# A table of due times, columns of its own for every expert's list, and an earlier source for the early gather

## The chip, the cores and the metric

The kernel runs on one core of one Trainium2 chip. The metric is the device time of one execution in microseconds, as a median over runs. The core has five engines that run side by side and wait for each other by semaphores: TensorE (PE: matmuls), VectorE (DVE), ScalarE (ACT), GpSimd (POOL, which also issues the indirect DMAs) and SyncE (SP, which issues all other DMAs). Each works its instructions off in the order in which they were written.

## What is computed

Three stages, each on the output of the one before; 4 sequences of 768 tokens, 8 heads of 48 columns, all in float32:

```
for t in range(S):                                        # attention as a scan with complex decay
    S_re, S_im = (ar*S_re - ai*S_im + kv, ar*S_im + ai*S_re)
    y[:, :, t] = einsum('bhd,bhde->bhe', q[:, :, t], S_re)
x = x / rms(x) * rms_g                                    # dense layer, 3072 tokens, 384 -> 1536 -> 384
x = (silu(x @ w_gate) * (x @ w_val)) @ w_out
expert_idx = argmax(x @ w_gate2)                          # 8 experts, 384 -> 1024 -> 384, one for each token
for e in range(8):
    xe = x[expert_idx == e]
    out[expert_idx == e] = gate_w * (relu(xe @ w1[e]) @ w2[e])
```

## The kernel before

**Units.** The tokens go in 12 units of 256 (`U`, two chunks of 128). For each unit `elem` computes decays and phases (on ACT, DVE and POOL) and multiplies q and k by them; SP copies the result into `QK`, by heads; `attention` runs two chunks in `chunk`: scores, mask, state, output rows, their RMS factor (ten tiny operations on one column, L757 to L766) and a transpose into `xh` and `xl`, the high and low parts of the input of the dense layer. `dense` has 12 features, each a first step of 18 matmuls (L827), tanh on ACT, two products and a low part on DVE or POOL (L836 to L844), and a second step of 6 matmuls (L850) into two accumulators. `finish` stores the unit's rows and their 8 logits in `x2all` in DRAM (L882), finds each row's expert (L888 to L892, the one-hot `oh`), ranks the rows within their experts by matmuls (L899 to L902), and scatters each row's number into the lists `slots` (L921; one list for each chunk of a pair, so that two halves exist).

**Experts.** After unit 9 the largest expert so far is chosen as expert 0; its weights are loaded and split during the last unit. Half of its rows are taken *early*, from the rows known until then; the other half and the seven other experts, sorted by size, follow. `read_list` (L1059) loads both halves of a list from DRAM by SP and takes their minimum on DVE (L1068). `expert` gathers the rows by indirect DMAs on POOL (L1085), turns them (L1111), runs the first layer in 8 steps (L1129; results leave PSUM by ACT, L1136, and DVE, L1138, tile `ehl`; three PSUM banks), then the second (L1147), and scatters the results to the output by indirect DMAs on POOL (L1155), which read the same index tile. Weights of the next expert come through three raw buffers (SP, L1043 and L1045), split by ACT (L1050) and DVE (L1054) into h1, l1, h2, l2; two sets of weights alternate.

**The index tiles.** The early and the late list of expert 0 have tiles of their own; the seven others share three slots (L944), so that the list of expert 4 takes the place of expert 1's.

**The order.** `Plan` holds every step with the engines that can do it, its costs in us, its buffers and a due time. `issue` runs through a model of the five engines: it writes next the step that can start first, among equals the one that is due first, and so fixes the order on each engine. What a step costs, how long a result needs to land (`lag`) and when it is due (the numbers of `TUNE`) thus move instructions between places and, where a step has a choice, between engines; a negative number added to DVE's cost draws a step to DVE. `lock` marks steps of DVE and POOL that the model lets run one at a time.

## Time and profile before

| | us |
|---|---|
| median of 3 runs (lowest, highest) | 1008.8 (1007.71, 1011.72) |
| the profiled execution, its own time | 1006.66 |
| its span, first to last instruction | 1005.0 |
| TensorE busy (matmul) | 909.5 |
| VectorE, ScalarE, GpSimd busy | 642.2, 520.4, 197.5 |
| TensorE's granted clock, mean | 0.965 |

All rows come from the one profiled execution; 1.0 of granted clock is full speed. A wait in a row is the idle time of the engine just before an instruction, and the arrow names what ended it. The program falls into a start of some 75 us, the dense units to some 724 us, and the experts.

### The profile page before, as it was taken

What the parts mean: (1) busy time and instruction counts of PE and PEld (TensorE: products, weight loads), DVE (VectorE), ACT (ScalarE), POOL (GpSimd) and SP (SyncE); (2) the same over time, 40 slices, a digit from 0 to 9 for tenths busy, and PEclk for the clock granted to TensorE, in tenths of its full rate; (3) what the DMA queues carried; (4) which work ended last, traced back from release to release, by engine and by line L of the source; (5) the groups of instructions that cost most, each with busy time, mean ns of one, the idle gap of its engine ahead of it and who ended that gap; (6) DMA issues with size and microseconds to landing.
All of it is one profiled execution on the core that took longest, in us unless ns stands there. A gap on an engine that the chain in (4) does not pass through costs nothing. (4 is left out here: it accounts for less than half of the span.)

```text
span 1005.0 us, 18341 instructions
## 1 busy us (share of the span) xinstructions
PE 909.5 (91%) x6919; PEld 880.8 (88%) x6919; DVE 642.2 (64%) x1606; ACT 520.4 (52%) x1040; POOL 197.5 (20%) x265
## 2 busy tenths in 40 slices
PE   1869999999999999999989999999888968999994
PEld 1859999989999999899979999999878867999994
DVE  6899997777778696768577674655545523535510
ACT  8776766565646565646365652333325422534420
POOL 2244531020111101111000300000154112222111
PEclk9878999999999999999989999999999997999998
DMA  8835314423241515051505030012147413445301
GB/s 319 253 113 152 133 42 103 99 76 82 62 118 53 133 33 127 17 117 47 122 22 127 29 64 17 1 59 85 49 129 219 153 54 126 146 127 167 108 15 27
DMA packets 68639, 98.65 MB, mean 98 GB/s; under 512 B 16035, under 2 KB 49509, under 8 KB 68548
## 3 DMA queue, kind: packets, MB, share of 16 engines
q1 hardware_dynamic: 57860, 87.41, 30.8%
q0 software_dynamic: 10688, 10.04, 3.7%
q8 instruction: 55, 0.90, 0.4%
q14 instruction: 36, 0.29, 0.1%
HBM read 68.19 MB, written 10.55 MB: 78 GB/s over the span
## 5 line engine op out<-in xcount | busy, mean ns | idle before, releaser
L827 PE MATMUL m<-xh,w 128*128 128x256 f32 x1728 | 273.5, 286 | 8.5 <-DVE s L839 8.0
L827 PEld LDWEIGHTS m<-xh,w 128*128 128x128 f32 x1728 | 238.4, 193 | 10.7 <-DVE s L839 9.5
L850 PE MATMUL a<-wo,hh 128*128 128x392 f32 (+1 forms) x576 | 155.6, 351 | 1.6 <-ACT hh L842 1.1
L827 PE MATMUL m<-xl,w 128*128 128x256 f32 x864 | 151.1, 284 | 0.0
L827 PEld LDWEIGHTS m<-xl,w 128*128 128x128 f32 x864 | 124.7, 192 | 0.3 <-DVE xl L792 0.3
L834 ACT ACTIVATE s<-m 128x256 f32<-128x256 f32 x144 | 54.5, 381 | 100.1 <-PE m L827 58.5
L850 PEld LDWEIGHTS a<-wo,hh 128*128 128x128 f32 x576 | 98.7, 189 | 3.4 <-ACT hh L842 1.5
L850 PE MATMUL a<-wo,hl 128*128 128x392 f32 (+1 forms) x288 | 98.2, 341 | 0.0
L842 ACT ACTIVATE hh<-s 128x256 fp32r<-128x256 f32 x144 | 59.5, 416 | 71.1 <-PE a L850 56.8
L836 DVE SCALAR_TENSOR_TENSOR s<-s,m 128x256 f32<-128x256 f32 x144 | 59.2, 414 | 38.9 <-ACT s L834 38.6
L844 DVE TENSOR_TENSOR hl<-s,hh 128x256 fp32r<-128x256 f32 x144 | 65.6, 457 | 28.3 <-ACT hh L842 27.0
L1136 ACT ACTIVATE ehh<-m 128x384 fp32r<-128x384 f32 (+6 forms) x64 | 31.3, 490 | 60.4 <-PE m L1129 60.2
L1138 DVE SCALAR_TENSOR_TENSOR ehl<-m,ehh 128x384 fp32r<-128x384 f32 (+6 forms) x64 | 34.9, 554 | 40.3 <-ACT ehh L1136 40.1
L839 DVE SCALAR_TENSOR_TENSOR s<-s,m 128x256 f32<-128x256 f32 x144 | 59.3, 415 | 2.1
L1155 POOL DMA_INDIRECT out_dram<-eo,idxrest x24 | 30.8, 1282 | 137.6 <-ACT eo L1153 71.4
L1153 ACT ACTIVATE eo<-a,eg 114x384 f32<-114x384 f32 (+5 forms) x28 | 16.2, 580 | 78.1 <-PE a L1147 72.5
L921 POOL DMA_INDIRECT slots<-tid,sl x24 | 26.3, 1096 | 151.5 <-DVE cnt L916 147.8
L850 PEld LDWEIGHTS a<-wo,hl 128*128 128x128 f32 x288 | 54.1, 188 | 0.5 <-DVE hl L844 0.5
L665 PE MATMUL t<-QK 96*128 96x128 f32 x384 | 49.6, 278 | 0.0
L665 PEld LDWEIGHTS t<-QK 96*128 96x128 f32 x384 | 46.4, 192 | 1.2 <-issue 0.7
L1220 PE MATMUL a<-w,identr 128*128 128x384 f32 x96 | 22.6, 393 | 26.1 <-ACT w L411 24.1
L1220 PEld LDWEIGHTS a<-w,identr 128*128 128x128 f32 x96 | 19.9, 225 | 27.2 <-ACT w L411 24.6
(261 smaller groups left out, 1967.9 us busy)
## 6 DMA issues: line engine op xcount, KB each, us to landing
rawb<-in_w_dram SPq DMA_DIRECT2D x21, 512.0 KB, 4.1
rawb<-in_w_dram SPq DMA_DIRECT2D x28, 384.0 KB, 4.5
QK<-qk SPq DMA_DIRECT2D x24, 290.2 KB, 4.7
QK<-ee SPq DMA_DIRECT2D x24, 290.2 KB, 4.9
x2all<-x SPq DMA_DIRECT2D x13, 392.0 KB, 2.5
re<-in_a_re_dram SPq DMA_DIRECT2D x12, 384.0 KB, 3.8
im<-in_a_im_dram SPq DMA_DIRECT2D x12, 384.0 KB, 4.1
qk<-in_q_dram SPq DMA_DIRECT2D x12, 384.0 KB, 4.7
```

The lines of the kernel that those rows point to most:

```text
L665: TE.matmul(sc.t[:, i, :], lhsT=K(4 * g + i), rhs=Q(4 * g + i), start=True, stop=True)
L827: TE.matmul(ps.t[:, i, :], lhsT=W1[i, f * P // WB][k].t[:, part, fs], rhs=x.t[:, k, :], start=(n == 0), stop=(n == 3 * KD - 1))
L834: add((A, act(U)), lambda e: e.activation(s.t, ps.t[:, 0, :], AF.Tanh, scale=0.5), r=[ps], w=[s], due=dh, table=AF.Tanh)
L836: add((V, dve(U)), lambda e: e.scalar_tensor_tensor(out=s.t, in0=s.t, scalar=1.0, in1=ps.t[:, 0, :], op0=ALU.add, op1=ALU.mult), r=[s, ps] ...
L839: add((V, dve(U)), lambda e: e.scalar_tensor_tensor(out=s.t, in0=s.t, scalar=0.5, in1=ps.t[:, 1, :], op0=ALU.mult, op1=ALU.mult), r=[s, ps ...
L842: add((A, act(U)), lambda e: e.activation(hh.t, s.t, AF.Copy), r=[s], w=[hh], due=dh)
L844: lambda e: e.tensor_tensor(out=hl.t, in0=s.t, in1=hh.t, op=ALU.subtract), r=[s, hh], w=[hl], due=dh, lock=True)
L850: TE.matmul(acc[t].t[:, :wide], lhsT=h.t[:, ts_], rhs=WO[f].t[:, part, :wide], start=(f == 0 and n == 0), stop=(f == KF - 1 and n == 2))
L1136: add((A, act(N)), lambda e, f=f, ps=ps: e.activation(hh.t[:, f, :], ps.t, AF.Relu), r=[ps], w=[(hh, f)], due=d - 20)
L1138: add((V, dve(N)), lambda e, f=f, ps=ps: e.scalar_tensor_tensor(out=hl.t[:, f, :], in0=ps.t, scalar=0.0, in1=hh.t[:, f, :], op0=ALU.max, o ...
L1155: add((G, 1.05), lambda e, o=o, j=j: e.indirect_dma_start(out=out, out_offset=bass.IndirectOffsetOnAxis(ap=at(j), axis=0), in_=o.t, in_off ...
L1220: TE.matmul(fill.t, lhsT=identr, rhs=w.t[:, 0, :WB], start=True, stop=True)
```

## The change

- The nine lists (early, late, seven others) get columns of their own in one tile for each half; the three shared slots are gone.
- The early gather reads `x2all[:NT - U]` and depends in the plan on the rows of units 0 to 10 alone; the store of zeros into the last unit's rows at the start is gone.
- Costs in the plan: scan 1.92 us (from 6 times 0.20), phase 2.13, choose 1.0, place 0.7, tiny operations 0.1, totals and row copies 0.1 more; the lag of a scatter of numbers is 2.6 (from 2.0), of a gather 4.4 (from 2.2), of an output scatter 4.4 (from 2.0).
- All due times are new, and some choices: `RG=2` writes the ten tiny operations of units 0 and 1 as one step; `PE0`, `PE1` and the biases `MB`, `LB`, `RB`, `HB`, `EB` change which steps go ahead and whether DVE or POOL takes them.

```
-TUNE = dict(T0=143.38, PER=73.18, ..., PE0=0, PE1=0.45, RG=0, LB=0.29, EB=-1.55, RB=5.75, HB=-16.82, MB=1.05, ...
+TUNE = dict(T0=141.9, PER=75.64, ..., PE0=0.2, PE1=0, RG=2, LB=0.31, EB=-2.92, RB=13.33, HB=-12.38, MB=-0.22, ...
...
-    k_idx = {n: [Slots(e_right, f"idx{n}{i}", [P, NJ], I32, k) for i in range(NC)]
-             for n, k in (("early", 1), ("late", 1), ("rest", 3))}
+    k_idx = [Slots(e_right, f"idx{i}", [P, E + 1, NJ], I32) for i in range(NC)]
...
-    def read_list(name, x, lo, n, after):
-        both = [Buf(k, shape=[TPS[x], n]) for k in k_idx[name]]
+    lists = [Buf(k) for k in k_idx]
+    def read_list(x, row, lo, n, after):
+        at = [lambda b=b: b.t[:TPS[x], row, :n] for b in lists]
...
-                out=X.t[:, j, :], out_offset=None, in_=x2all,
-                r=[idx, X2ALL], w=[(X, j)], due=due(-30), lag=2.2, after=after)
+        rows, src = ([(X2ALL, u) for u in range(NU - 1)], x2all[:NT - U]) if rooms is rooms0 else ([X2ALL], x2all)
+                out=X.t[:, j, :], out_offset=None, in_=src,
+                r=[IDX] + rows, w=[(X, j)], due=due(-30), lag=4.4, after=after)
...
-        dma(lambda e: e.dma_start(x2all[NT - U:NT, :].rearrange("(c p) e -> p c e", p=P), zr.t),
-            U * XW * 4, r=[zr], w=[(X2ALL, NU - 1)], due=40)
```

**Expert 4's list, SyncE.** The place is expert 2's first layer. `rawb` are weight loads, `idxrest` a list load; DMASW are the semaphores of POOL's DMAs, DMAHW those of SP's. Before:

```order
L1043 DMA rawb_9759<-in_w_dram 128x1024 [waits DMAHW0_49,DVE_49]
L1064 ISA
L1064 DMA idxrest_9773<-slots_58 128x3 [waits DMASW6_49,DMASW7_49,DMASW5_49,DMASW4_49]
L1043 ISA
L1043 DMA rawb_9776<-in_w_dram 128x1024 [waits DMAHW1_49,DVE_49]
```

And in the changed kernel:

```order
L1041 DMA rawb_9760<-in_w_dram 128x1024 [waits DMAHW4_49,DVE_49]
L1041 ISA
L1041 DMA rawb_9775<-in_w_dram 128x1024 [waits DMAHW5_49,DVE_49]
L1041 ISA
L1041 DMA rawb_9806<-in_w_dram 128x1024 [waits DMAHW6_49,DVE_49]
```

The list load between the first two weight loads is gone; all lists now stand in the hand-over, some 70 rows earlier. On DVE, at the same place, the minimum goes from between two of expert 2's evictions:

```order
L1054 TENSOR_TENSOR l2b_9738<-rawb_9754,h2b_9729 128x768 [waits DMAHW2_49,Activation_49]
L1068 TENSOR_TENSOR idxrest_9773<-idxrest_9773,idxrest_9123 128x3 [waits DMASW7_49,DMASW6_49,DMAHW4_49,DMASW5_49,DMASW4_49]
L1138 SCALAR_TENSOR_TENSOR ehl_9756<-m_9781,ehh_9750 128x456 [waits Activation_49]
L1138 SCALAR_TENSOR_TENSOR ehl_9756<-m_9795,ehh_9750 128x456 [waits Activation_49]
L1138 SCALAR_TENSOR_TENSOR ehl_9756<-m_9814,ehh_9750 128x456 [waits Activation_49]
```

In the changed kernel `l2b` is followed by the evictions at once.

**The hand-over, TensorE.** The end of the last unit, where the ranking (`tri`, `ones`: L899 to L902) meets the early half of expert 0 (`h1a`, `l1a`). Before:

```order
L850 MATMUL a_8625<-wo_1846,hl_8822 128x392
L1111 MATMUL t_8848<-ident,x_8704 128x123 x2
L899 LDWEIGHTS ones
L899 MATMUL t_8865<-cnt,ones 128x8
L902 LDWEIGHTS tri
L902 MATMUL t_8865<-oh_8858,tri 128x8
```

In the changed kernel:

```order
L849 MATMUL a_8624<-wo_1764,hl_8821 128x392
L1132 MATMUL m_8852<-xh_8829,h1a_8288 128x246 x3
L1132 MATMUL m_8852<-xl_8841,h1a_8288 128x246 x3
L1132 MATMUL m_8852<-xh_8829,l1a_8292 128x246 x3
L1132 MATMUL m_8865<-xh_8829,h1a_8288 128x246 x3
L1132 MATMUL m_8865<-xl_8841,h1a_8288 128x246 x3
L1132 MATMUL m_8865<-xh_8829,l1a_8292 128x246 x3
L1132 MATMUL m_8886<-xh_8829,h1a_8288 128x246 x3
L1132 MATMUL m_8886<-xl_8841,h1a_8288 128x246 x3
L1132 MATMUL m_8886<-xh_8829,l1a_8292 128x246 x3
L898 LDWEIGHTS ones
L898 MATMUL t_8900<-cnt,ones 128x8
```

Three steps of nine matmuls now stand between the last dense matmul and the ranking.

**The start, VectorE.** The tiny operations of unit 0's second chunk (tile `rs`) among those of unit 1 (`ee`, `re`, `im`) and weight conversions (`raw`, `wo`). Before:

```order
L758 TENSOR_SCALAR rs_709<-rs_709 128x1
L532 COPY ee_666<-ee_666 128x3x2
L539 TENSOR_TENSOR ee_666<-ee_666 128x256 x3
L759 TENSOR_SCALAR rs_709<-rs_709 128x1
L406 SCALAR_TENSOR_TENSOR raw_354<-wo_216,raw_354 128x384
L761 TENSOR_TENSOR rs_709<-magic,rs_709 128x1
L401 SCALAR_TENSOR_TENSOR raw_496<-raw_496,wo_390 128x384
L762 TENSOR_SCALAR rs_709<-rs_709 128x1
```

In the changed kernel:

```order
L757 TENSOR_SCALAR rs_667<-rs_667 128x1
L758 TENSOR_SCALAR rs_667<-rs_667 128x1
L760 TENSOR_TENSOR rs_667<-magic,rs_667 128x1
L761 TENSOR_SCALAR rs_667<-rs_667 128x1
L763 SCALAR_TENSOR_TENSOR rs_667<-rs_667 128x1
```

The ten stand together, and unit 1's long operations behind them.

## Rows read from the trace of the kernel before

**Rows 1.** The page, busy tenths in 40 slices of 25.1 us: TensorE's total, TensorE, VectorE.
```profile
PE 909.5 (91%) x6919; PEld 880.8 (88%) x6919; DVE 642.2 (64%) x1606; ACT 520.4 (52%) x1040; POOL 197.5 (20%) x265
...
PE   1869999999999999999989999999888968999994
...
DVE  6899997777778696768577674655545523535510
```

**Rows 2.** TensorE's waits: line waited for, us in total, times, longest us.
```profile
PE m L1129 <- DVE ehl L1138: 16.9, 3, 12.8
PE m L827 <- DVE s L839: 8.0, 5, 3.8
```

**Rows 3.** TensorE's timeline (start us, us), and the window behind it (busy, PEclk).
```profile
833.60 1.51 PE L1129 MATMUL m<-exh,h1a 128*128 128x456 f32 x3 [12.79 <-DVE ehl L1138]
...
833.60:841.00 7.40, 7.40 (x24) 6.61 (x25) 1.91 (x4) 1.38 (x3) 2.92 (x3) 0.62 0.57 194
```

**Rows 4.** VectorE's timeline at that place.
```profile
832.84 0.16 DVE L1068 TENSOR_TENSOR idxrest<-idxrest,idxrest 128x3 int32<-128x3 int32 x1 [14.82 <-DMA idxrest<-slots]
```

**Rows 5.** SyncE's timeline at that place (issues alone).
```profile
812.97 0.35 SPq L1043 DMA_DIRECT2D rawb<-in_w_dram  x1
831.08 0.34 SPq L1064 DMA_DIRECT2D idxrest<-slots  x1
831.69 0.92 SPq L1043 DMA_DIRECT2D rawb<-in_w_dram  x2
```

**Rows 6.** POOL's timeline at that place.
```profile
823.15 1.64 POOL L1155 DMA_INDIRECT out_dram<-eo,idxrest  x1 [6.91 <-issue]
```

**Rows 7.** DMA issues, whole run: count, KB each, median us from issue to landing.
```profile
rawb<-in_w_dram SPq DMA_DIRECT2D x28, 384.0 KB, 4.5
...
ex<-x2all,idxrest POOLq DMA_INDIRECT x24, 7.5
out_dram<-eo,idxrest POOLq DMA_INDIRECT x24, 4.9
```

**Rows 8.** A window over later experts: us, then PE, PEld, DVE, ACT, POOL busy.
```profile
850.00:960.00 110.00, 110.00 (x638) 108.54 (x637) 50.53 (x92) 47.85 (x87) 25.95 (x22) 1.00 0.41 126
```

**Rows 9.** TensorE's timeline at the hand-over: its three waits.
```profile
725.59 0.17 PE L902 MATMUL t<-oh,tri 128*128 128x8 bf16 x1 [2.00 <-DVE oh L892]
...
747.05 1.73 PE L1111 MATMUL t<-ident,ex 123*128 123x123 f32 x6 [4.87 <-DMA idxrest<-slots]
...
760.25 0.63 PE L1129 MATMUL m<-exh,h1a 128*128 128x246 f32 x3 [3.37 <-DVE ehl L1138]
```

**Rows 10.** SyncE's and POOL's timelines at the hand-over: the late list and its first gather.
```profile
732.11 0.77 SPq L1064 DMA_DIRECT2D idxlate<-slots  x2
...
737.85 1.44 POOL L1085 DMA_INDIRECT ex<-x2all,idxlate  x1 [8.63 <-DVE idxrest L1068]
```

**Rows 11.** A window of early first-layer steps; a subtraction of weights on VectorE's timeline.
```profile
732.64:736.76 4.12, 4.12 (x37) 4.12 (x37) 2.76 (x16) 1.13 (x3) 0.00 (x0) 1.00 0.08 2
...
748.13 1.22 DVE L1054 TENSOR_TENSOR l1b<-rawb,h1b 128x1024 fp32r<-128x1024 f32 x1
```

**Rows 12.** TensorE's timeline, the first dense matmul.
```profile
75.18 1.09 PE L827 MATMUL m<-xh,w 128*128 128x256 f32 x3 [0.46 <-ACT xh L788]
```

**Rows 13.** VectorE's timeline, first and last of the second chunk's ten tiny operations.
```profile
67.02 0.15 DVE L758 TENSOR_SCALAR rs<-rs 128x1 f32<-128x1 f32 x1 [0.30 <-ACT y L753]
...
72.59 0.15 DVE L765 SCALAR_TENSOR_TENSOR rs<-rs 128x1 f32<-128x1 f32 x1
```

**Rows 14.** Groups by line: gain products (count, busy us, mean ns, idle before).
```profile
L586 DVE TENSOR_TENSOR ee<-qk,ee 128x768 f32<-128x768 f32 x24 | 23.5, 988 | 4.6 <-ACT ee L546 4.6
```

**Rows 15.** VectorE's and POOL's timelines at 58 us.
```profile
58.57 0.95 DVE L765 SCALAR_TENSOR_TENSOR rs<-rs 128x1 f32<-128x1 f32 x1
...
58.26 1.25 POOL L416 TENSOR_TENSOR w<-raw,w 128x384 fp32r<-128x384 f32 x1
```

**Rows 16.** Groups by line: the centring on POOL.
```profile
L539 POOL TENSOR_TENSOR ee<-ee 128x256 f32<-128x256 f32 x21 | 12.9, 639 | 51.5 <-DVE ee L532 51.5
```

More of the change, by code (lines that the diff above doesn't have):

```diff
@@ L28 @@
 TABLE_LOAD = 1.3
-TUNE = dict(T0=143.38, PER=73.18, FT=4.13, A0=68.94, A1=-49.43, A2=-21.78, E0=-117.9, E1=66.72, E2=94.44,
-            E3=115.52, CG=0.23, CO=255.09, LC=-54.51, NRAW=6, AHEAD=6, DH=22.42, FI=-69.19, RP=-13.39, TOL=0,
-            S2L=47.73, NS=3, NH=3, HOP=0.2, W1=133.05, ATP=2, PA0=0, PA1=0, PE0=0, PE1=0.45, RG=0, LB=0.29,
-            EB=-1.55, RB=5.75, HB=-16.82, MB=1.05, TB=25.48, AX=1, EE=-32.55, EL=7.09, BEG=0.7, DL=2, FN=8,
-            FF=23)
+TUNE = dict(T0=141.9, PER=75.64, FT=4.32, A0=71.68, A1=-61.52, A2=-18.6, E0=-150.88, E1=65.4, E2=78.3, E3=75.68,
+            CG=8.52, CO=243.96, LC=-56.68, NRAW=6, AHEAD=6, DH=24.1, FI=-65.62, RP=-25.83, TOL=0, S2L=45.45,
+            NS=3, NH=3, HOP=0.2, W1=131.99, ATP=2, PA0=0, PA1=0, PE0=0.2, PE1=0, RG=2, LB=0.31, EB=-2.92,
+            RB=13.33, HB=-12.38, MB=-0.22, TB=26.62, AX=1, EE=-22.83, EL=9.31, BEG=0.7, DL=2, FN=8, FF=23)
 HOP = TUNE["HOP"]
@@ L527, in scan @@
                                          initial=0.0, op0=ALU.add, op1=ALU.subtract)
-        at((V, 6 * dve(C)), scan, r=[ta, tb], w=[(ee, "m")], lock=True)
+        at((V, 1.92), scan, r=[ta, tb], w=[(ee, "m")], lock=True)
         at([(G, pool2(N3)), (V, dve(N3))],
@@ L735, in keep_rows @@
                     e.tensor_copy(yT[s], yt.t[s])
-            at([(A, act(4 * C)), (V, dve(4 * C))], keep_rows, r=[yt], w=[(YT, n)])
+            at([(A, act(4 * C)), (V, dve(4 * C) + 0.1)], keep_rows, r=[yt], w=[(YT, n)])
         def turn_rows(e):
@@ L910, in place @@
             e.tensor_copy(sl.t, mx.t)
-        add((V, 0.9), place, r=[rk, oh], w=[t1, mx, sl], due=due)
+        add((V, 0.7), place, r=[rk, oh], w=[t1, mx, sl], due=due)
         def count(e):
@@ L1057, in load_weights @@
         return W
-    def read_list(name, x, lo, n, after):
-        both = [Buf(k, shape=[TPS[x], n]) for k in k_idx[name]]
+    lists = [Buf(k) for k in k_idx]
+    def read_list(x, row, lo, n, after):
         due = due_e(x, -30)
-        for x_, sl in zip(both, slots):
-            dma(lambda e, x_=x_, sl=sl: e.dma_start(x_.t, sl[bass.ds(which[x] * NT + lo, n * TPS[x]), :].rearrange(
-                "(p j) o -> p (j o)", j=n)), 2e3, r=[SLOTS], w=[x_], due=due,
-                after=after + [told[x]])
-        a, o = both
-        add((V, 0.1), lambda e: e.tensor_tensor(out=a.t, in0=a.t, in1=o.t, op=ALU.min), r=both, w=[a], due=due)
-        return a
+        at = [lambda b=b: b.t[:TPS[x], row, :n] for b in lists]
+        for b, t, sl in zip(lists, at, slots):
+            dma(lambda e, t=t, sl=sl: e.dma_start(t(), sl[bass.ds(which[x] * NT + lo, n * TPS[x]), :].rearrange(
+                "(p j) o -> p (j o)", j=n)), 2e3, r=[SLOTS], w=[(b, row)], due=due, after=after + [told[x]])
+        a, o = at
+        add((V, 0.1), lambda e: e.tensor_tensor(out=a(), in0=a(), in1=o(), op=ALU.min),
+            r=[(lists[1], row)], w=[(lists[0], row)], due=due)
+        return row
     begun = []
@@ L1078, in expert @@
         N = n * TP
+        rows, src = ([(X2ALL, u) for u in range(NU - 1)], x2all[:NT - U]) if rooms is rooms0 else ([X2ALL], x2all)
+        IDX = (lists[0], idx)
         def at(j):
-            return idx.t[:, j:j + 1]
+            return lists[0].t[:TP, idx, j:j + 1]
         X, g = Buf(k_x, shape=[TP, n, XW]), Buf(k_g, shape=[TP, n, E + 1])
@@ L1157, in expert @@
                 in_=o.t, in_offset=None, bounds_check=NT - 1, oob_is_err=False),
-                r=[o, idx], due=d, lag=2.0)
+                r=[o, IDX], due=d, lag=4.4)
     with tc.manual_schedule():
@@ L1240 @@
             if u + 1 == NU:
-                early = read_list("early", 0, 0, NE, [to_right])
+                early = read_list(0, 0, 0, NE, [to_right])
                 expert(0, Wn, early, NE, rooms0, lambda i: due_e(0, i) - TUNE["EE"], [to_right])
@@ L1251 @@
         add((V, 2.0), sort, r=[MORE, HOT], w=[PERM], due=due_moe(NU, 0) - 60)
-        late = read_list("late", 0, EARLY, NJ - NE, [to_right])
+        late = read_list(0, E, EARLY, NJ - NE, [to_right])
         expert(0, Wn, late, NJ - NE, rooms, lambda i: due_e(0, i), [to_left])
@@ L1255 @@
             W = load_weights(x_, [to_left])
-            idx = read_list("rest", x_, 0, NJS[x_], [to_right])
+            idx = read_list(x_, x_, 0, NJS[x_], [to_right])
             expert(x_, W, idx, NJS[x_], rooms, lambda i, x_=x_: due_e(x_, i), [to_left])
```

10 lines of the change are left out of this document (5 added, 5 removed).

## The prediction

> **What bounds the kernel now.** I read the page first. TensorE is busy for 909.5 of 1005.0 us, and the slices show where it isn't: at the very start, in slices 29 to 34 (the hand-over to the experts) and in the last [rows 1]. TensorE bounds the kernel and its matmuls are the same before and after, so the question is which of its idle stretches go and which come. The table of its waits names them by releaser [rows 2]: 12.8 us in one piece behind a VectorE eviction `ehl` (L1138); the dense steps' waits for evictions are 8.0 us in five, the longest 3.8.
>
> I followed the 12.8 us back, engine by engine. TensorE's timeline has it at 820.81 to 833.60, in the first layer of expert 2 (456 rows) [rows 3]: three PSUM banks are full, and VectorE doesn't empty them. VectorE's timeline says why: it stood for 14.82 us at L1068, the minimum of the two halves of expert 4's list, whose second half had not landed, with the evictions queued behind it [rows 4]. SyncE issued that list load at 831.08, though its previous instruction was at 812.97; two weight loads then followed at once, so they had waited behind it [rows 5]. POOL's timeline gives the cause: the last scatter of expert 1 went out at 823.15 for 1.64 us [rows 6], a scatter lands 4.9 us after its issue in the median [rows 7], and until then the index tile that it reads can't be overwritten. That list takes the slot of expert 1 (three slots for seven lists). So **the chain is scatter landing, list load, minimum, eviction, matmul**, and nothing in it is arithmetic. After the wait the granted clock is 0.62 in the mean of 833.60 to 841.00, between the levels of 1.2 and 2.4 GHz [rows 3].
>
> **Term 1, own columns.** The nine lists get columns of their own. In the order of the changed kernel no list load waits for a scatter (their waits are all on SyncE's own rings), and expert 2's evictions have no minimum between them. The wait goes whole: 12.79 us, and with it 7.4 x (1 - 0.62) = 2.8 us of slow clock [rows 3], together **-15.6 us**. What is late next here? The weight loads of expert 4, which stood behind the list; they now follow their own buffers, which VectorE frees before it reaches the place of the old wait. From 850 to 960 the same pattern, with shorter list waits, leaves TensorE busy for 110.00 of 110.00 us [rows 8]; I take that as what this stretch is without the stall. Bounds: -15.6, and -11 should one weight load's landing, 4.5 us [rows 7], show in its place.
>
> Here the Trainium skill weighs in ("DMA: Bandwidth & Descriptors", section on the anatomy of a DMA from GpSimd): such a DMA costs about 2.0 us fixed plus its bytes. By it the list would have been free at some 826.8, four us sooner, and the term would be an estimate of -11.5. The trace disagrees: 4.9 us for a scatter, and 7.5 us for a gather [rows 7].
>
> **Term 2, the hand-over.** Dense work ends at 723.59. TensorE then waits 2.00 us for the one-hot [rows 9], ranks, and SyncE reads the late list at 732.11; POOL starts the late gathers at 737.85 [rows 10], and TensorE, out of early work, stands still until 747.05 [rows 9]. Now three steps of the early expert (27 matmuls) stand ahead of the ranking. A stretch of 36 such matmuls takes 4.12 us [rows 11], so they take 3.1 us and cover the wait. But the ranking comes 1.1 us later, and so may the gathers. TensorE has 12 second-layer matmuls more done when it meets the late turn, 1.4 us at the 0.114 us of rows 11 and more as they are longer; but nothing then covers the eviction of the turned rows. I take -2 us: the wait for the one-hot, the rest against each other. The 3.37 us wait at 760.25 [rows 9] is again VectorE in order (expert 1's gate, which waits for a gather, ahead of evictions); two evictions now stand ahead of that gate: -1 us. Bounds of both: -10.2 (all three waits go) and +3.5 (three subtractions of expert 1's weights, 1.22 us each [rows 11], now stand ahead of the late rows' low part, where one did). Term: **-3 us**.
>
> The early gather reads `x2all[:NT - U]` and the zero fill of the last unit's rows is gone. The gather was already ordered after unit 10 alone, so I cost this at nothing; what covers the gather is the last unit's dense work, and without it some 7.5 us of landing [rows 7] would show. The last unit's row store no longer waits for it, and it wasn't late.
>
> **Term 3, the start.** The first dense matmul runs at 75.18, 0.46 us after its input [rows 12]. That input waits for the ten tiny RMS operations of the second chunk, which VectorE spread over 67.02 to 72.74 between long ones [rows 13]. With RG=2 the ten stand together: 10 x 0.15 = 1.5 us instead of 5.7, **4.2 us** sooner. Moreover the work of unit 1 ahead of the first dense eviction shrinks, three gain products (L586) fewer alone: 3 x 0.99 = 3.0 us [rows 14]. Both only defer work of VectorE, which is busy for 90% or more of slices 3 to 6, until 150 us [rows 1]; so most is given back. Bounds -9 (all kept) and +3 (unit 1's preparation, now later, stops attention). Term: **-3 us**.
>
> Here a rule speaks against the change. Beside a POOL subtraction from 58.26 to 59.51 a one-column VectorE operation (L765) took 0.95 us [rows 15], which elsewhere takes 0.15 [rows 13]. The changed order has seven such subtractions (L416) on POOL before unit 1's factors, not four. The Trainium skill ("SBUF — State Buffer", section on who interferes with whom) has it that a VectorE operation with two SBUF inputs and a GpSimd one that reads SBUF exclude each other for a whole instruction. By that rule three more of the row's 1.25 us take up to 3.8 us from VectorE (an estimate), and term 3 would be some +0.8. The row agrees, in one place; how often the two meet is not seen in it, so the term stays and its bound holds this.
>
> **Term 4, the middle.** In six units the centring `middle` (L539) moves from POOL to VectorE: 18 instructions of 0.64 us there [rows 16], at most 11.5 us onto VectorE, which has 6 to 8 tenths to do in those slices [rows 1]. Fewer matmuls stand between a unit's last turn of y and its first dense step: counted in the order, 174 in unit 6 before (and attention besides), 54 now. That is less reserve, not a wait. I take **0**; below, all of the 8.0 us of rows 2 could go, above, as much could come.
>
> Of the planner's other numbers (durations of scan, totals, gates, lags) none adds an instruction; they act through the order alone, and are in the terms above. The tail, three scatters one after another behind the last matmul, stands in the same order: 0.
>
> **Sum.** -15.6 - 3 - 3 + 0 = -21.6 us against the profiled execution's 1006.66 us: 985.1. The median of the runs shown is 1008.8, 2.1 us above that execution: **987 us**.
>
> **The rivals.** *Stall only* (0.28): the order's other moves cancel. Then 1008.8 - 15.6 = 993. For it: terms 2 and 3 are small, and each has a bound on the other side. *More than I count* (0.10): the three hand-over waits go whole (-10.2 for -3) and the start keeps 6 of its 9 us: 987 - 7 - 3 = 977. *The wait moves* (0.07): all seven later lists are now loaded during the hand-over, between weight loads that wait for VectorE, and their minima stand on VectorE ahead of the late half's evictions. If a list sits behind a weight load as it did before, TensorE pays one wait of rows 3 again: 993 + 15.6 = 1008. Against it: no scatter is in that chain now. *Slower: attention late at every unit* (0.06): the reserve ahead of units 3 to 6 falls to 18 to 60 matmuls (at 0.114 us some 2 to 7 us), VectorE has `middle` besides, and the first step then waits for xl. At the 3.8 us of rows 2 six such stops in eleven units give 993 + 23 = 1016; it is slower from the sixth on, and with four about even. For it: VectorE is in order, and one late operation has that price. Against it: no present wait of that kind shows. *It doesn't do what it says* (0.01): should the columns of one tile be treated as one buffer, list loads would still wait for scatters. The order shows they don't. The forecast itself has 0.48.
>
> A measurement of this kernel can't tell less than about 0.5% (5 us) from no change. Faster by more: 0.48 + 0.28 + 0.10 = 0.86; within: 0.07 + 0.01 = 0.08; slower: 0.06. The range must drop no more than 2 in 10: I leave out the two cases at 1008 and above and the far end of the bounds below (-15.6 - 10 - 9 = -35 gives 974), and hold the forecast, the stall-only case and its bound of -11 with +3.5 of term 2 (about 1001): 975 to 1002.
>
> **What would show it.** In the changed profile: no list load later than the hand-over and no VectorE wait of over 3 us for one; expert 2 without a gap, clock 1.00 throughout the experts (term 1). No wait for the one-hot, and the turn of the late rows still waiting 3 to 6 us (term 2). The first dense matmul at 66 to 71 us (term 3). Waits of the dense steps for evictions of 0 to 16 us together (term 4). Wrong, if TensorE's idle time between 760 and 960 stays over 10 us, or if waits for xh or xl appear at the starts of units.

## The result and the profile after

| | before | changed |
|---|---|---|
| median of 4 runs (lowest, highest), us | 1008.25 (1003.58, 1011.72) | 975.51 (974.43, 980.38) |
| ratio, 95% interval | | 0.9688 (0.9636, 0.9739) |
| span of the profiled execution, us | 1005.0 | 972.7 |
| TensorE busy, us | 909.5 | 901.4 |
| TensorE idle: 0 to 100 us / 100 to 700 us / 700 us to the last matmul / tail | 35.7 / 22.0 / 25.0 / 12.8 | 42.2 / 6.4 / 9.9 / 12.8 |

The change takes 33 us, where the forecast had 22; the new time lies half a microsecond inside the lower end of the stated range. The last row of the table is the one to read: it is each stretch less TensorE's busy time in it, from the windows below. The start became worse, the units lost nearly three quarters of their idle time, and the experts lost 15 us. TensorE's busy time also fell by 8.1 us for the same 6919 matmuls. That is the granted clock: 1.00 for 0.99 in the units and 0.97 for 0.96 behind them, in the windows below. These busy times are those of one execution each, and executions of one and the same kernel differ in their clock too (last section).

The page of the changed kernel, where the lines of [rows 1] stand now:

```profile
PE 901.4 (93%) x6919; PEld 877.0 (90%) x6919; DVE 642.2 (66%) x1612; ACT 527.8 (54%) x1050; POOL 186.4 (19%) x249
...
PE   0867999999999999999999999999987999999994
...
DVE  5889897858787868786968586646545543554510
...
PEclk9978899999999999999999999999997999999998
```

Windows of the changed kernel (stretch, then PE, PEld, DVE, ACT, POOL busy with counts, granted clock, DMA share, GB/s):

```profile
0.00:100.00 100.00, 57.79 (x394) 54.69 (x394) 82.83 (x165) 73.26 (x134) 33.87 (x74) 0.88 0.60 196
100.00:700.00 600.00, 593.61 (x5085) 580.35 (x5085) 444.28 (x1210) 349.57 (x724) 78.81 (x119) 1.00 0.31 77
700.00:959.90 259.90, 249.96 (x1444) 242.01 (x1442) 115.07 (x238) 104.39 (x191) 71.49 (x54) 0.97 0.42 123
765.00:835.00 70.00, 70.00 (x382) 66.59 (x381) 31.92 (x51) 29.63 (x50) 17.09 (x14) 1.00 0.46 141
```

And of the kernel before:

```profile
0.00:100.00 100.00, 64.35 (x457) 60.50 (x458) 85.05 (x179) 75.85 (x144) 32.84 (x70) 0.88 0.66 208
100.00:700.00 600.00, 577.95 (x4914) 561.77 (x4914) 435.86 (x1172) 333.97 (x691) 88.05 (x138) 0.99 0.29 74
700.00:992.20 292.20, 267.20 (x1552) 258.49 (x1550) 121.31 (x256) 110.00 (x204) 74.33 (x57) 0.96 0.38 112
```

In the first 100 us the changed kernel runs 63 matmuls fewer, though VectorE is nearly as busy (82.83 us for 85.05). From 100 to 700 us it is the other way round: 171 more, at full clock. From 765 to 835 us, where the 12.8 us stood [rows 3], TensorE is never idle.

TensorE's waits in the changed kernel (line waited for, us in total, times, longest), against [rows 2]:

```profile
PE a L1221 <- POOL w L412: 25.1, 1, 25.1
PE t L781 <- ACT y L776: 7.3, 5, 5.0
PE m L826 <- ACT w L410: 5.1, 1, 5.1
PE m L1132 <- DVE ehl L1141: 4.0, 2, 3.2
...
PE m L826 <- DVE s L838: 0.5, 2, 0.3
```

The first line is the idle time ahead of the first matmul (19.8 us before). The dense steps' waits for evictions fell from 8.0 to 0.5 us. New are a wait of 5.0 us for `y` and one of 5.1 us for a dense weight, both in the start. The hand-over in TensorE's timeline, against [rows 9]:

```profile
727.32 0.30 PE L1114 MATMUL t<-ident,ex 123*128 123x123 f32 x1 [2.70 <-DMA idx<-slots]
729.21 1.29 PE L1114 MATMUL t<-ident,ex 123*128 123x123 f32 x5 [1.59 <-DMA ex<-x2all,idx]
...
741.49 1.00 PE L1132 MATMUL m<-exh,h1a 128*128 128x246 f32 x3 [3.20 <-DVE ehl L1141]
```

The wait for the one-hot is gone, the late turn waits 4.3 us in two pieces (4.87 before), and the wait for `ehl` is 3.20 us (3.37 before).

### The profile page after: what moved, and what is told of

It is laid out like the page before. It is cut to its first block, busy times and chain, and to the rows that moved or that the text cites. A ratio compares the mean times of both kernels' runs of the same rounds, so it can differ in the third digit from the quotient of the medians.

```text
span 972.7 us, 18324 instructions
## 1 busy us (share of the span) xinstructions
PE 901.4 (93%) x6919; PEld 877.0 (90%) x6919; DVE 642.2 (66%) x1612; ACT 527.8 (54%) x1050; POOL 186.4 (19%) x249
## 5 line engine op out<-in xcount | busy, mean ns | idle before, releaser
L826 PE MATMUL m<-xh,w 128*128 128x256 f32 x1728 | 276.3, 286 | 6.0 <-ACT w L410 5.1
L843 DVE TENSOR_TENSOR hl<-s,hh 128x256 fp32r<-128x256 f32 x144 | 62.3, 437 | 33.5 <-ACT hh L841 32.9
L835 DVE SCALAR_TENSOR_TENSOR s<-s,m 128x256 f32<-128x256 f32 x144 | 59.0, 414 | 36.0 <-ACT s L833 35.3
L1158 POOL DMA_INDIRECT out_dram<-eo,idx x28 | 37.6, 1344 | 152.0 <-ACT eo L1156 47.1
L664 PE MATMUL t<-QK 96*128 96x128 f32 x384 | 52.0, 279 | 1.7 <-DMA QK<-ee 1.7
L1221 PE MATMUL a<-w,identr 128*128 128x384 f32 x96 | 21.7, 382 | 27.4 <-POOL w L412 25.1
L1221 PEld LDWEIGHTS a<-w,identr 128*128 128x128 f32 x96 | 19.3, 217 | 27.9 <-POOL w L412 25.1
```

Source lines behind the costliest of these rows:

```text
L664: TE.matmul(sc.t[:, i, :], lhsT=K(4 * g + i), rhs=Q(4 * g + i), start=True, stop=True)
L826: TE.matmul(ps.t[:, i, :], lhsT=W1[i, f * P // WB][k].t[:, part, fs], rhs=x.t[:, k, :], start=(n == 0), stop=(n == 3 * KD - 1))
L835: add((V, dve(U)), lambda e: e.scalar_tensor_tensor(out=s.t, in0=s.t, scalar=1.0, in1=ps.t[:, 0, :], op0=ALU.add, op1=ALU.mult), r=[s, ps] ...
L843: lambda e: e.tensor_tensor(out=hl.t, in0=s.t, in1=hh.t, op=ALU.subtract), r=[s, hh], w=[hl], due=dh, lock=True)
L1158: add((G, 1.05), lambda e, o=o, j=j: e.indirect_dma_start(out=out, out_offset=bass.IndirectOffsetOnAxis(ap=at(j), axis=0), in_=o.t, in_off ...
L1221: TE.matmul(fill.t, lhsT=identr, rhs=w.t[:, 0, :WB], start=True, stop=True)
```

## The experiments

The order on each engine is fixed when the kernel is written, so it can be recorded. In six kernels below (start_before, units_before, experts_before, loads_first, first_30us_before, weights_swapped) the plan doesn't choose: the changed kernel is written in a given list of steps, each with its engine. At step 740 (some 165 us) and at step 2660 (some 665 us) the two orders have done the same steps but for three and for none, so that they can be joined there. This is the edit (`ORDER` is the list; the ten tiny operations of units 0 and 1 are single steps in it):

```
+        turn = [(self.steps[int(w.rstrip("."))], w.endswith(".")) for w in ORDER]
         left = len(self.steps)
         while left:
             cand = []
-            for s in ready:
+            for s, other in turn:
+                if s.wait:
+                    continue
...
-                for e, c, *bias in s.engs:
+                for e, c, *bias in [s.engs[other]]:
```

| kernel | median (lowest, highest), us | ratio to before (95%) | idle, as above | TensorE busy |
|---|---|---|---|---|
| own_columns | 992.43 (988.18, 995.83) | 0.9827 (0.9794, 0.9860) | 34.2 / 23.9 / 13.4 / 12.2 | 910.0 |
| start_before | 970.94 (970.09, 973.21) | 0.9627 (0.9600, 0.9653) | 33.9 / 9.3 / 10.9 / 12.5 | 902.3 |
| units_before | 1002.97 (998.80, 1006.82) | 0.9924 (0.9896, 0.9952) | 41.4 / 22.4 / 13.1 / 12.6 | 912.1 |
| experts_before | 977.15 (975.57, 981.42) | 0.9692 (0.9663, 0.9722) | 42.4 / 6.8 / 12.9 / 12.3 | 900.6 |
| due_times_only | 1016.48 (1013.17, 1021.26) | 1.0079 (1.0049, 1.0108) | 36.6 / 21.1 / 30.0 / 12.2 | 913.4 |
| durations_only | 1001.07 (999.18, 1002.33) | 0.9915 (0.9891, 0.9940) | 35.3 / 12.5 / 24.6 / 12.9 | 913.5 |
| old_due_times | 985.11 (980.68, 985.42) | 0.9745 (0.9717, 0.9774) | 41.1 / 14.9 / 15.0 / 12.1 | 900.3 |
| loads_first | 992.34 (990.51, 997.08) | 0.9845 (0.9815, 0.9874) | 33.9 / 22.0 / 14.9 / 12.5 | 905.6 |
| scan_phase_only | 984.38 (983.73, 988.43) | 0.9796 (0.9772, 0.9821) | 39.0 / 18.1 / 14.3 / 12.0 | 899.4 |
| small_costs_only | 1003.34 (998.02, 1008.24) | 0.9962 (0.9941, 0.9984) | 40.7 / 22.9 / 13.7 / 12.5 | 912.6 |
| first_30us_before | 980.97 (979.74, 983.96) | 0.9753 (0.9732, 0.9774) | 41.4 / 8.7 / 11.0 / 12.3 | 904.7 |
| weights_swapped | 977.71 (975.37, 982.11) | 0.9708 (0.9687, 0.9729) | 42.6 / 7.3 / 12.2 / 12.7 | 905.6 |

The kernel before stood beside the first four at 1009.57 us (median), beside the next four at 1009.55, beside the last four at 1007.32. Differences between two of these kernels are taken from medians, and the spread within one kernel says that under some 4 us they mean little. The ratios are not ratios of the medians, and a difference taken from them can come out some 5 us otherwise; where that matters, both are given. Idle and busy times are those of one profiled execution.

### own_columns

```
+        if s.name.startswith("idxrest"):
+            if not hasattr(s, "whole"):
+                s.whole, s.row = s.where[0].tile([s.shape[0], 7, s.shape[1]], s.dtype, name=s.name, tag=s.name, bufs=1), 0
+            self.t = s.whole[:self.shape[0], s.row, :self.shape[1]]
+            s.row += 1
+            return
```

This stands in `Buf.place` of the kernel before: the plan still counts three slots and makes the same order, only the buffers differ.

> The kernel before, with the order of every engine unchanged; only the seven later lists get columns of their own, so that no list load has to wait for a scatter. Theory (term 1 is the own columns alone, whatever the order): the wait of 12.8 us at the first layer of expert 2 goes with its slow clock, 1008.3 - 15.6 = 992.7 us, within 2.5; TensorE's idle time from 763 us to the last matmul under 1 us. Rival (the list load then waits in SyncE's queue behind a weight load, or the weight load is what is late): the wait shrinks to 4 to 12 us and the time is 997 to 1008. Second rival (the order of the change is needed for the gain): 1005 or more.

Measured: ratio 0.9827, which is 17 us off (14 to 21 by the interval). The two kernels can be laid beside each other from the matmul behind the wait for `ehl` in the hand-over to the last one, 1227 matmuls in the same order. The kernel before, then own_columns:

```profile
760.25:992.20 231.95, 218.35 (x1227) 211.57 (x1227) 93.58 (x164) 89.33 (x158) 52.48 (x41) 0.96 0.38 116
```

```profile
764.20:981.60 217.40, 216.10 (x1227) 210.50 (x1227) 94.37 (x164) 90.22 (x158) 53.20 (x41) 0.99 0.41 123
```

TensorE is idle for 1.3 us there, one wait at 787 us, where it was idle for 13.6 before. From 763 us on, the stretch of the expectation, it is 2.5 us with the end of the wait for `ehl`, not under 1. List load and minimum stand where they stood. The stretch is 14.6 us shorter, 12.3 us of it idle time and 2.3 us clock, against 12.8 and 2.8 in term 1. That is a better measure of term 1 than the 17 us: the spans of the two profiled executions differ by only 11.2 us, since this execution of own_columns came to the stretch 4 us later, and the kernel's six runs lie in two groups, 988.2 to 990.4 and 994.5 to 995.8 us, with the median between them. So term 1 is the buffers alone, the order of the change isn't needed for it, and in this order nothing took the wait's place.

### units_before

`ORDER` is the change's up to step 740, that of before from there to step 2660, the change's behind it.

> The changed kernel, whose steps 741 to 2660 (units 2 to 10, some 165 to 665 us) are written in the order of the kernel before; start, hand-over and experts as in the change. Theory (the due times of the units, not the lists, bring the larger part: idle 16.4 us less and the clock's loss of some 5.8 us gone): 975.5 + 20 = 995 us, within 4, with the two waits of 3.8 and 2.5 us for evictions near 500 and 527 us back. Rival (the units gain because of how the start leaves VectorE): 975 to 983. Second rival (half of each): 983 to 991.

Measured: 1002.97 us, 27 us slower than the change (24 by the two ratios), more than any theory had. Both waits are back:

```profile
515.30 0.62 PE L986 MATMUL m<-xh,w 128*128 128x256 f32 x3 [4.21 <-DVE s L998]
537.47 1.01 PE L986 MATMUL m<-xh,w 128*128 128x256 f32 x3 [2.53 <-DVE s L998]
```

The spans differ by 28.9 us: idle time by 18.1 (16.0 of it in the units, 3.2 behind them), busy time by 10.8 (912.1 against 901.4). **The order of units 2 to 10 is the largest part of the change**, and over a third of what it is worth is clock: in the kernel before, the 3.8 us stop at 502 us is followed by nine microseconds at a mean granted clock of 0.69, between its levels of 1.2 and 2.4 GHz, without any idle time in them:

```profile
506.00:515.00 9.00, 9.00 (x66) 8.58 (x67) 5.05 (x13) 6.01 (x10) 0.00 (x0) 0.69 0.00 0
```

Busy time doesn't follow idle time in every kernel, though: durations_only (below) is idle for 10 us less than the kernel before and busy for 4 us more.

### experts_before

`ORDER` is the change's up to step 2660, and that of before from there, lists included (they have own columns here too).

> The changed kernel, whose last 893 steps (the last unit, hand-over and experts) are written in the order of the kernel before, with the lists in columns of their own. Theory (the order at the hand-over is worth little: idle time of 9.9 us against 11.4 before, same clock): 975.5 + 1.5 = 977 us, within 2.5. Rival (ranking behind three steps of the early expert and the lists loaded early are worth what term 2 allowed): 980 to 986. Second rival (own columns need the early loads): a wait of over 4 us in the experts, 982 to 990.

Measured: 977.15 us, 1.6 us slower than the change, less than the runs tell apart; TensorE's idle time behind 700 us is 3.0 us more. The wait for the one-hot (2.00 us) and the late turn's 4.89 us are back, and little else:

```profile
700.00:962.70 262.70, 249.76 (x1456) 241.98 (x1454) 115.86 (x241) 104.61 (x193) 72.19 (x54) 0.99 0.42 123
```

### start_before

`ORDER` is that of before up to step 740, and the change's behind it.

> The changed kernel, whose first 740 steps (the start and units 0 and 1, to some 165 us) are written in the order of the kernel before, all later ones in the order of the change. Theory (the changed start is worse: its idle time to 100 us is 42.2 us against 35.7, with about 1 us more of slow clock): 975.5 - 7.5 = 968 us, within 3. Rival (a start only moves work of VectorE: what it gains is given back before 300 us): 973 to 977. Second rival (the gain of the later units comes from what the changed start does ahead): slower than the change, 980 or more.

Measured: 970.94 us, as the theory had it and faster than both kernels by medians (its interval and the change's, 0.9600 to 0.9653 and 0.9636 to 0.9739, overlap a little; the three kernels with the changed units and the changed start, in weights_swapped but for two conversions, are at 975.5 or over). So the changed start costs about 5 us. The loss, in the stretch from 60 to 100 us, of start_before:

```profile
60.00:100.00 40.00, 32.53 (x265) 30.67 (x262) 38.99 (x90) 27.14 (x59) 13.51 (x18) 0.80 0.45 122
```

and of the changed kernel:

```profile
60.00:100.00 40.00, 25.63 (x163) 24.17 (x163) 38.84 (x82) 24.34 (x52) 14.61 (x19) 0.74 0.31 100
```

VectorE is full in both (39 of 40 us), but TensorE does 102 matmuls fewer in the changed order. Its waits say what differs. In the kernel before, 18 turns of output weights (`wo`) stand ahead of the first dense matmul, and TensorE waits for two conversions among them, 5.9 us in all (start_before has the same two waits):

```profile
69.87 0.47 PE L439 MATMUL t<-identr,wo 128*128 128x128 f32 x1 [3.50 <-POOL wo L413]
72.73 1.33 PE L439 MATMUL t<-identr,wo 128*128 128x128 f32 x5 [2.39 <-DVE wo L416]
```

In the changed kernel 6 such turns stand there; TensorE now waits for `y` and `xl` instead, 6.6 us in all:

```profile
66.62 0.90 PE L781 MATMUL t<-ident,y 128*128 128x128 f32 x3 [4.97 <-ACT y L776]
70.73 1.10 PE L826 MATMUL m<-xl,w 128*128 128x256 f32 x3 [1.66 <-DVE xl L791]
```

The waits for conversions come all the same, behind the first dense matmul: 5.07 us, shown next, and 1.52 us at 99 us. So the idle time of this stretch (14.4 us against 7.5) grew by about what the waits for `y` and `xl` are.

### weights_swapped and first_30us_before

The changed kernel's 5.07 us wait, followed back: TensorE's row, and ACT's ahead of it, of the changed kernel.

```profile
95.47 0.58 PE L826 MATMUL m<-xh,w 128*128 128x256 f32 x1 [5.07 <-ACT w L410]
...
91.94 1.28 ACT L580 ACT_TABLE_LOAD   x1
...
93.35 0.92 ACT L581 ACTIVATE ta<-ta,halfpi 128x768 f32<-128x768 f32 x1
94.17 0.83 ACT L589 ACTIVATE re<-re 128x768 f32<-128x768 f32 x1
94.91 0.51 ACT L410 ACTIVATE w<-raw 128x384 fp32r<-128x384 f32 x1
```

A dense weight's high part stands on ACT behind unit 1's cosine and sine. Two conversions were exchanged in `ORDER` (steps 213 to 218 and 248 to 253):

```
+m = {249: 214, 248: 213, 250: 215, 251: 216, 252: 217, 253: 218}
+m.update({v: k for k, v in m.items()})
+ORDER = [(m.get(q, q), other) for q, other in ORDER]
```

> The changed kernel in its own order, but two conversions of dense weights change places in it: the one for which TensorE waits 5.07 us at 95 us goes into the places of the one that stands ahead of it and is due later (so it gets its scratch buffer some 10 us sooner, and its last step on ACT stands ahead of unit 1's cosine with its table load, not behind). Theory (this one late conversion is most of what the changed start loses): the wait goes to under 1.5 us, 975.5 - 4 = 971.5 us, within 2. Rival (the next conversion is then late, or the time gained is given back while VectorE catches up): the wait moves, 974 to 978.

Measured: 977.71 us. That wait is gone, and 5.9 us in two others came for it, in the same kernel's timeline:

```profile
96.14 0.47 PE L598 MATMUL t<-identr,wo 128*128 128x128 f32 x1 [1.58 <-POOL wo L572]
100.95 1.33 PE L598 MATMUL t<-identr,wo 128*128 128x128 f32 x5 [4.34 <-DVE wo L575]
```

The rival holds: with VectorE full, one conversion brought forward makes another late. In the other kernel `ORDER` is that of before for the first 120 steps alone.

> The changed kernel whose first 120 steps (to some 32 us) alone are in the order of the kernel before. Theory (the first matmul at 25.1 us instead of 19.8 costs nothing, since the first dense step waits for attention; what the changed start loses is lost between 60 and 100 us): first matmul at 20 us, time 973 to 978. Rival (those 5.3 us are the loss): 971 us as with the whole start of before, within 1.5.

Measured: 980.97 us, a miss for both. The first matmul is back at 19.5 us and the first dense one comes at 71.5 (68.0 in the change), behind a new stop:

```profile
42.49 0.55 PE L844 MATMUL t<-ident,QK 96*128 96x96 f32 x4 [3.01 <-ACT AT L828]
```

Here an earlier first matmul gained nothing by itself, and with the join at 32 us the kernel became slower. The wait of 5.0 us for `y` stayed in both of these kernels. Which of the start's many moves makes it worse stays open: only the whole start of before was shown to repair it.

### due_times_only, durations_only, old_due_times

The change of the plan in its two halves. due_times_only is the kernel before with the new `TUNE`; durations_only is the kernel before with the other numbers of the diff (scan, phase, choose, place, tiny operations, totals, row copies, three lags); old_due_times is the changed kernel with the old `TUNE`.

> The kernel before with the changed table of due times and choices alone; costs and lags in the plan, shared slots, zero store and the source of the early gather as before. Theory (the due times and choices carry the gain of the units; the list wait is a matter of the shared slots): idle time from 165 to 700 us falls from 20 us to under 8, the start is that of the change, one list wait of 8 to 15 us stays or moves: 1009.6 - 27.5 + 4.6 = 987 us, within 6. Rival (the measured durations carry it, and due times searched for them are worth nothing without): 1000 us or more, idle time from 165 to 700 us over 14.

> The kernel before with the changed costs and lags in the plan alone (scan 1.92, phase 2.13, tiny operations 0.1 and the others; lags 2.6 and 4.4); due times, shared slots, zero store and source of the early gather as before. Theory (due times): idle time from 165 to 700 us stays over 14, time 1009.6 within 6. Rival (measured durations): idle time from 165 to 700 us under 8 and 982 to 992 us. The lag of 4.4 us could by itself move the list load of expert 4 and shorten its wait by up to 5 us; that alone would show at 820 us.

> The changed kernel with the due times and choices of the kernel before; own columns, source of the early gather, costs and lags as in the change. Theory (due times carry the units): 992.4 us as with own columns alone, within 5, idle time from 165 to 700 us over 14, no list wait. Rival (durations carry them): 971 to 980.

Measured: 1016.48, 1001.07 and 985.11 us; idle time from 165 to 700 us 11.7, 7.1 and 11.4 us. My theory fell, and the rival fits none of the three in both time and idle time. The new due times alone make the kernel slower by 0.5 to 1.1%, with a list wait of 13.8 us still there. The durations alone make it 0.6 to 1.1% faster, also with a list wait (11.5 us), and bring the units' idle time to 12.5 us. Durations with own columns give 985 us, some 24 us of the 33; the new due times add the last 10 us on top of these by medians, 6 by the ratios, 8.5 us of them in the units' idle time (14.9 to 6.4). Own columns and durations add up: 17 and 8.5 apart, 24.5 together.

From 200 us on, either half by itself takes away half or more of the idle time up to 700 us: 19.2 us before, 9.6 with the due times, 3.5 with the durations, 5.0 in the change. What each half pays alone, it pays elsewhere: from 100 to 200 us 11.5 and 9.1 us (2.9 before, 1.4 in the change), and the due times also behind 700 us (30.0 against 25.0). Why only the two together keep that stretch free stays open.

In old_due_times a list wait is back in the hand-over, though every list has its own columns. VectorE's row and TensorE's:

```profile
747.03 0.16 DVE L1068 TENSOR_TENSOR idx<-idx,idx 128x3 int32<-128x3 int32 x1 [6.96 <-DMA idx<-slots]
750.69 1.00 PE L1133 MATMUL m<-exh,h1a 128*128 128x246 f32 x3 [6.62 <-DVE ehl L1142]
```

SyncE had issued the second half of that list at 738.41, between loads of weights; why it landed only some 8.6 us later stays open. Its minimum stands ahead of the evictions, as in the kernel before. So own columns free the list load of the scatter alone; where the load and the minimum stand still counts.

### scan_phase_only and small_costs_only

old_due_times once more, with its numbers divided in two:

```
-        at((V, 6 * dve(C)), scan, r=[ta, tb], w=[(ee, "m")], lock=True)
+        at((V, 1.92), scan, r=[ta, tb], w=[(ee, "m")], lock=True)
...
-        at((V, 3 * dve(U) + 0.3), phase, r=[im, CARRY], w=[re, CARRY], lock=True)
+        at((V, 2.13), phase, r=[im, CARRY], w=[re, CARRY], lock=True)
```

are in the first and not in the second; the small costs and the lags the other way round.

> The changed kernel with the due times and choices of the kernel before, as in old_due_times, and of the measured durations only the two long ones: scan 1.92 us for 1.22, phase 2.13 us for 1.31. The other costs and the lags are those of before. Theory (the planner gains because it now reserves VectorE for the 1.5 us by which each unit's two scans were taken too short): as old_due_times, 985 us within 5, idle time from 200 to 700 us about 10. Rival (the many small costs or the lags carry it): 992 or more, idle time from 200 to 700 us over 15.

> The complement: the changed kernel with the due times and choices of before, scan and phase at their old 1.22 and 1.31 us, but the small costs (0.1 us for a tiny operation, 0.1 more for totals and row copies, choose 1.0, place 0.7) and the lags 2.6 and 4.4 of the change. Theory (scan and phase carry the gain): 992 us as with own columns alone, within 5, idle time from 200 to 700 us over 15. Rival (small costs and lags): 985 within 4. If both of these runs come to about 985, any better fit of the plan to the chip does it; if both to 992, only the two together.

Measured: 984.38 and 1003.34 us; idle time from 200 to 700 us 8.5 and 20.4 us. In windows of the kernel before, of scan_phase_only and of small_costs_only:

```profile
200.00:700.00 500.00, 480.84 (x4044) 468.50 (x4044) 350.86 (x955) 265.72 (x542) 58.79 (x95) 0.99 0.28 70
```

```profile
200.00:700.00 500.00, 491.45 (x4177) 481.07 (x4177) 356.78 (x974) 272.23 (x562) 63.83 (x97) 1.00 0.30 74
```

```profile
200.00:700.00 500.00, 479.61 (x4003) 466.71 (x4002) 350.09 (x945) 263.61 (x540) 62.27 (x98) 0.98 0.29 71
```

By medians the two long costs do by themselves what all of them do (984.4 and 985.1 us); by the ratios (0.9796 and 0.9745) they do some 5 us less. The small ones alone leave this idle time as it was (19.2 before, 20.2 in own_columns). They miss the 992 within 5, but their 1003 us are not lost in the units: against own_columns 6.5 us of idle time came in the first 100 us. With the due times of before, idle time from 200 to 700 us is 19.2 to 20.4 us in the three plans with the old costs of scan and phase (before, own_columns, small_costs_only) and 3.5 to 10.4 us in the three with the new ones (durations_only, scan_phase_only, old_due_times). Each is one plan, so the sizes can hold luck; the sign is the same in every pair. The rows of the kernel before say how wrong the old costs were:

```profile
L526 DVE TENSOR_TENSOR_SCAN ee<-ta,tb 128x128 f32<-128x128 f32 x72 | 26.3, 433 | 0.4
L561 DVE TENSOR_TENSOR_SCAN re<-im,carry 128x256 f32<-128x256 f32 x24 | 16.9, 760 | 4.3 <-ACT im L551 4.3
L561 DVE TENSOR_TENSOR_SCAN re<-im 128x256 f32<-128x256 f32 x12 | 7.4, 670 | 0.9 <-ACT im L551 0.9
```

That is (26.3 + 16.9 + 7.4) / 12 = 4.2 us of VectorE for each unit, where the plan had 1.22 + 1.31 = 2.5. What comes late in such a plan shows in TensorE's waits from 200 to 700 us, first of small_costs_only, then of scan_phase_only:

```profile
PE t L782 <- ACT y L777: 9.8, 6, 2.3
```

```profile
PE t L782 <- ACT y L777: 3.9, 8, 1.5
```

`y` is ACT's product with the RMS factor, and that comes from ten VectorE operations in order. That these come late because VectorE was booked too short is argued from the two sets of rows; no run moved them alone.

### loads_first

In the kernel before, the stop at 502 us has an immediate cause that can be moved alone. Its rows on SyncE and ACT:

```profile
485.11 4.05 SPq L610 DMA_DIRECT2D QK<-qk  x5
...
490.59 5.09 SPq L610 DMA_DIRECT2D QK<-ee  x4
495.72 0.58 SPq L484 DMA_DIRECT2D re<-in_a_re_dram  x1
...
502.51 0.84 ACT L505 ACTIVATE ta<-re 128x768 f32<-128x768 f32 x1 [4.54 <-DMA re<-in_a_re_dram]
```

The `tanh` of a dense step stands behind that square on ACT. In the whole order of before on the changed code, each such load was put ahead of copies, at the first place where its buffer is free (`last` is the last step that uses it):

```
+ORDER.remove(load)
+ORDER.insert(last + 1, load)
```

> The order of the kernel before on every engine but SyncE, lists in columns of their own (as in own_columns; also without the zero store, and the early gather from finished rows). On SyncE the load of each unit's a_re stands as soon as its buffer is free, ahead of five to ten copies into QK, in units 3 to 11. Theory (the 3.7 us stop of TensorE near 505 us is ACT standing in order at the square of a_re, whose load was issued behind those copies at 0.9 us each): ACT's wait at that line falls from 15.6 us to under 5, the stop near 505 us goes with the slow clock behind it, 992.4 - 3.7 - 2.8 = 986 us, within 2.5; the stop of 2.5 us near 528 us stays. Rival (another operation is late at the same place, or the copies now come late): 990 to 994, and a wait for QK or for evictions in its place.

Measured: 992.34 us, the same as own_columns; a miss. ACT's wait at that line fell as expected, from

```profile
  DMA re<-in_a_re_dram: 16.9, 5
```

in own_columns to

```profile
  DMA re<-in_a_re_dram: 4.1, 2
```

and the 3.7 us stop is gone, but units' idle time is 22.0 us against 23.9: near 400 us TensorE now waits at the turns of QK (1.1 and 1.0 us), whose copies stand behind the load. As in the start, one stop taken away by hand came back elsewhere in part. This kernel also has the zero store gone and the early gather from finished rows; together with the moved loads they are worth nothing that can be measured, and no run has them alone.

## Why the prediction was right and wrong

The time lay in the range (975 to 1002), half a microsecond from its lower end, and the sign was right. The working behind it was right in one term of four and near in a second:

| term | predicted | measured | by |
|---|---|---|---|
| 1, own columns | -15.6 | -17 (14 to 21); -14.6 in the stretch itself | own_columns |
| 2, hand-over | -3 | -1.6, under the noise; -3.0 in idle time | experts_before |
| 3, start | -3 (-9 to +3) | +5 | start_before |
| 4, units ("middle") | 0 (-8 to +8) | -27 with the changed start | units_before |

The terms taken in the change's surroundings don't add to the 33 us: the changed start costs some 10 us with the units of before (own_columns 992 against units_before 1003) and 5 with the new ones. One after another they do: 1009.6 before, 992.4 with own columns (-17), 970.9 with the new order of units and hand-over besides (-21.5), 975.5 with the changed start (+4.6).

**Term 1** held in each step: the chain scatter, list load, minimum, eviction, matmul was cut by the buffers alone. The weight loads didn't take its place. What could be saved was the wait as the row had it, 12.79 us, whatever one scatter costs. The estimate by the Trainium skill's fixed 2.0 us ("DMA: Bandwidth & Descriptors", section on the anatomy of a DMA from GpSimd), -11.5, is 3 us short of the 14.6 measured in the stretch. The rival "the wait moves" didn't come about in the changed kernel, but it stands in old_due_times, with 6.6 us.

**Term 2** was right in its waits (one-hot gone, the late turn 4.3 us where 3 to 6 was said) and near in size. Of the wait behind `ehl` 1 us was to go; it lost 0.2. One list minimum waited 3.64 us in the hand-over, where I had ruled out 3; TensorE didn't show it.

**Term 3** failed at this step: "The first dense matmul runs at 75.18 ... 4.2 us sooner". It came 7.2 us sooner, as foretold (67.98, where 66 to 71 was said), and the start lost 5 us all the same. Not the ten operations alone had held it: before, TensorE was still busy with turns of output weights, and waiting for their conversions, when it reached the turn of `y`; twelve of these turns now stand behind. The first dense matmul is the wrong mark in a stretch where VectorE is full: TensorE waits 5.0 us for `y` ahead of it, and the conversions put off cost 5.07 us at 95 us. I had written that both moves "only defer work" and that most is given back; more than all was. The mark to price was TensorE's idle time up to 100 us. The bound of -9 had no working either: the two items come to 7.2. The rule on GpSimd that I weighed and left out pointed the right way (last section), for the term would have been +0.8 by it.

**Term 4** is the main miss, and it failed at two sentences. "None adds an instruction; they act through the order alone, and are in the terms above": they were in no term. The planner's costs for scan and phase were 2.5 us where the profile had 4.2 in each unit, in two groups of rows that I had before me and didn't hold against the code. The new due times do their part besides: with the new costs in place they bring the idle time of the units from 14.9 to 6.4 us. And "below, all of the 8.0 us of rows 2 could go": the bound counted one releaser and left out the other 14 us of idle time in the units (waits for `y`, `yT`, `AT`, the one-hot) and the clock behind the stops, which is 10.8 us of busy time between units_before and the change. The rival of that place, attention late at every unit, was the opposite of what happened; the lead over the first step did shrink, and of the waits for `xl` that I had named as a sign of being wrong only one of 1.66 us came, in the first unit.

So the forecast was 11 us off, and that the time still lay in the range was luck: two errors of opposite sign, +8 in the start and some -19 to -27 in the units, met a term that was right. The case "more than I count" had 977 us, but for other reasons (the hand-over's waits).

## What to carry to other kernels

Where a planner fixes the order, hold its costs against the profile, operation by operation, before pricing any move: here two long operations with wrong costs were worth more than all small ones. Price a re-planning by all the idle time of the stretch and the slow clock behind it, not by the waits of one name. Moving one item in a stretch with one full engine didn't repair it here; the mark of such a stretch is the idle time of the engine that bounds the kernel, not the first arrival. And compare a stretch between the same two instructions: two executions of one kernel can differ by as much as the effect.

## What the runs showed of the hardware that I had not expected

Every stretched VectorE operation stands beside GpSimd. Of the operations of the kernel before, 40 took over 0.25 us more than the median of their own line and shape, 20.9 us above it in all, and each of the 40 overlaps an instruction on POOL (of all VectorE instructions 22% do); in the changed kernel 36 and 20.6 us, again each beside POOL. The waits of 2.5 us at 527 us (and in units_before at 537) have two of them ahead: these `hl` take 1.0 us each, 0.42 in the median. VectorE's row and POOL's, kernel before:

```profile
525.88 2.04 DVE L844 TENSOR_TENSOR hl<-s,hh 128x256 fp32r<-128x256 f32 x2
...
525.86 0.83 POOL L570 TENSOR_SCALAR ta<-re 128x768 f32<-128x768 f32 x1 [6.58 <-DVE re L561]
526.78 0.88 POOL L572 TENSOR_SCALAR ta<-ta 128x768 f32<-128x768 f32 x1
```

The rule of the Trainium skill that the prediction weighed ("SBUF — State Buffer", section on who interferes with whom) agrees in direction. The total is nearly the same before and after, but not its place: in the first 100 us it rose from 5.4 to 7.8 us (17 operations for 12), from 100 to 700 us it fell from 15.5 to 12.8. So it can be part of what the start lost; no run moved it alone.

Executions of one kernel differ in their granted clock, and their time goes with it. The three shorter runs of own_columns (988.2 to 990.4 us) had a mean clock of 0.977 to 0.982, the three longer ones (994.5 to 995.8 us) 0.970, with the same instructions in the same order. The nine runs of units_before go the same way: 998.8 to 1000.1 us at 0.968 to 0.969, 1003.0 to 1006.8 us at 0.962 to 0.965. Not every difference is of this kind: in experts_before the longest run, 981.4 us, has the highest clock, 0.977. What makes the clock differ from one execution to the next no run here shows.
